# A fused attention and expert kernel: its program ordered by a model of the engines inside the kernel, and two blocks that take d_ff in halves

## The chip, the cores and the metric

The kernel runs on one core of a Trainium2 chip. The metric is device time in microseconds (us), the median of several runs. The engines named below: PE (TensorE, matrix products), DVE (VectorE), ACT (ScalarE), POOL (GpSimd), and SP, whose queue issues most of the transfers (DMAs).

## The reference

Attention in which keys and values are first averaged over groups of 8 positions, then an expert layer whose activation is a rational function:

```python
# attention: q, k, v are (8, 8, 576, 64): images, heads, positions, head size
k_p = k.reshape(B, H, Sp, 8, D).mean(axis=3)        # 72 pooled positions
v_p = v.reshape(B, H, Sp, 8, D).mean(axis=3)
scores = scale * np.matmul(q, k_p.transpose(0, 1, 3, 2))
scores = scores - np.max(scores, axis=-1, keepdims=True)
attn = np.exp(scores)
attn = attn / (np.sum(attn, axis=-1, keepdims=True) + 1e-09)
x = np.matmul(attn, v_p)       # laid out as 4608 tokens x 512
# expert: w_in 512 x 2048, w_out 2048 x 512 (both arrive as 8-byte floats)
h = x @ w_in
P = a[0] + a[1]*h + a[2]*h*h + a[3]*h*h*h
Q = 1.0 + np.abs(b[0])*np.abs(h) + np.abs(b[1])*h*h
out = (P / (Q + 1e-6)) @ w_out
```

## The kernel before

*Tiling.* The 4608 tokens are 18 blocks of 256, d_ff is 8 slices of 256. A unit (i, u) is block i with slice u, 144 in all. Products are made in three passes of a high and a low part (high x high, low weights x high, high weights x low), so `mm1` (L403) is 24 matmuls into one bank `ph`, and `mm2` (L448) 12 matmuls of 512 columns into the two banks `po` of the block's output, which gather over all 8 slices.

*Between them* `rational` (L414) computes the activation of a unit: three ACT reads (L421 to L423), a POOL product (L424), two DVE operations on `ph` (L425, L426), Ln and Exp on ACT into the bank `rp` (L432, L433), three DVE operations (L434, L436, L438), then the split into `gh` (ACT, L440) and `gl` (POOL, L441). mm2 of a unit stands LAG = 3 units behind its mm1.

*Weights.* `fetch` and `fetch_out` load 1 MB for each slice of w_in and w_out; `decode` (L160) turns 8-byte floats into a high and a low part with two ACT, two DVE (L168, L171) and one POOL operation per tensor (L166, L176, L177). A slice's two tensors are called a pair of weights below.

*Attention.* Per image, `prep_k` pools k (DVE, L233) and `prep_v` pools v (POOL, L199, L202; masks by ACT and DVE, L275 to L284). Per block, `attention` runs twice, on 128 tokens each: transposes of q (pq, L323), scores (ps, L338) with maximum and subtraction on DVE, exponential, sum and reciprocal, scaling (L352), the remainder `er` (L360, L361), transposes `pm` and `pr`; then `values` (L379) makes x in a high and a low part.

*Order.* The start, until block 0's x, is written out by hand in `tc.manual_schedule()` (L519 to L559). After that the units are emitted in the order of the list `order` (L564): blocks 0 and 1 together, block 1 two slices behind block 0, through all 8 slices, then block after block. Beside each unit a share of the next block's preparation and attention is emitted (`background`), and during block 0 the decoding of the slices ahead; a scheduler of the language then orders each engine's instructions when the program is built. At run time each engine takes its instructions in that order.

Of the kernel before, what the change touches and what calls it, by code (L numbers as in the profile page):

```python
# [13 lines left out]
AX = mybir.AxisListType  # L14


@with_exitstack
def tile_pooled_attention_then_rational_moe(
# [43 lines left out]
    ps_a = ctx.enter_context(tc.tile_pool(name="ps_a", bufs=2, space=PS))
# [16 lines left out]
    def make_masks():
# [15 lines left out]
        bands = tmp.tile([P, 4], F32, tag="tmp", name="bands")  # L95
# [20 lines left out]

    def make_scalars():
        for i in range(4):
            nc.gpsimd.tensor_scalar(out=abn[:, i:i + 1], in0=ab[:, i:i + 1],
                                    scalar1=-WS ** -i, scalar2=None, op0=ALU.mult)  # L120
        nc.scalar.activation(abn[:, 4:6], ab[:, 4:6], AF.Abs)

# [9 lines left out]


# [4 lines left out]
    def stage_tile(name, at=None):  # L138
        if at is None:
            return stage.tile([P, 1024], F32, tag="st", name=name)  # L140
        if at // 2 not in halves:
            halves[at // 2] = cpool.tile([P, 2, CW], F32, tag=spare[at // 2], name=name)
        return halves[at // 2][:, at % 2, :]

    w_in32, w_out32 = w_in.bitcast(I32), w_out.bitcast(I32)
    raw, win, wout = {}, {}, {}

    def fetch(u):
        w = raw[f"win{u}"] = cpool.tile([P, 2 * CW], F32, tag=f"win{u}", name=f"rwin{u}")
        nc.sync.dma_start(  # L150
            w.bitcast(I32).rearrange("p (k x) -> p k x", x=4 * P),
            w_in32[:, u * 4 * P:(u + 1) * 4 * P].rearrange("(k p) x -> p k x", p=P))

    def fetch_out(u):
        w = raw[f"wout{u}"] = cpool.tile([P, 2 * CW], F32, tag=f"wout{u}", name=f"rwout{u}")
        nc.sync.dma_start(
            w.bitcast(I32).rearrange("p (f x) -> p f x", f=2),
            w_out32[u * 2 * P:(u + 1) * 2 * P, :].rearrange("(f p) x -> p f x", p=P))

    def decode(kind, u):  # L160
        name = f"{kind}{u}"
        words = raw.pop(name).bitcast(I32).rearrange("p (n t) -> p n t", t=2)
        hw, lw = words[:, :, 1], words[:, :, 0]
        m = dec.tile([P, CW], F32, tag="m", name=f"m_{name}")
        mi = m.bitcast(I32)
        nc.scalar.activation(m, hw.bitcast(F32), AF.Prelu, scale=2.0 ** -111, alpha=-2.0 ** 32)  # L166
        yield
        nc.vector.tensor_scalar(out=mi, in0=mi, scalar1=3, scalar2=None,  # L168
                                op0=ALU.logical_shift_left)
        yield  # L170
        nc.vector.scalar_tensor_tensor(out=mi, in0=lw, scalar=29, in1=mi,  # L171
                                       op0=ALU.logical_shift_right, op1=ALU.bitwise_or)
        yield
        w = cpool.tile([P, 2, CW], F32R, tag=name, name=name)
        (win if kind == "win" else wout)[u] = w
        nc.scalar.copy(w[:, 0, :], m)  # L176
        nc.gpsimd.tensor_tensor(out=w[:, 1, :], in0=m, in1=w[:, 0, :].bitcast(F32),  # L177
                                op=ALU.subtract)
        yield

    def load_win(u):
        return decode("win", u)

    def load_wout(u):
        return decode("wout", u)


    kpT = [cpool.tile([P, NJ, 2 * SP], F32, tag=f"kpT{i}", name=f"kpT{i}") for i in range(2)]
    vm = [[cpool.tile([P, NJ, P], F32R, tag=f"vm{s}{i}", name=f"vm{s}{i}")
           for s in range(2)] for i in range(2)]  # L190
    vr = [cpool.tile([P, NJ, D], F32R, tag=f"vr{i}", name=f"vr{i}") for i in range(2)]
    for i in range(2):
        nc.gpsimd.memset(kpT[i], 0.0)

    def pool_rows(dst, st):

        w = st.shape[2] // 2
        while w > D:
            nc.gpsimd.tensor_tensor(  # L199
                out=st[:, :, 0:w], in0=st[:, :, 0:w], in1=st[:, :, w:2 * w], op=ALU.add)  # L200
            w //= 2
        nc.gpsimd.tensor_tensor(  # L202
            out=dst, in0=st[:, :, 0:w], in1=st[:, :, w:2 * w], op=ALU.add)

    def place(n, ks, j0, j1):

        pk = ps_a.tile([P, j1 - j0, SP], F32, tag="pa", name=f"pk{n}_{j0}")
        for j in range(j0, j1):
            nc.tensor.transpose(
                pk[:, j - j0, :], ks[:, 2 * j:2 * j + 2, :].rearrange("s h d -> s (h d)"),  # L210
                ident[:SP, :SP])
        for hh in range(2):
            rows = slice(hh * D, (hh + 1) * D)
            nc.scalar.activation(
                kpT[n % 2][rows, j0:j1, hh * SP:(hh + 1) * SP], pk[rows], AF.Copy,
                scale=1.0 / G)

    def prep_k(n):
        ks = tmp.tile([P, H * D], F32, tag="tmp", name=f"ks{n}")[:SP].rearrange("s (h d) -> s h d", h=H)

        def load(j):
            st = stage_tile(f"st_k{n}_{j}", j if n == 0 else None)
# [6 lines left out]
        if n == 0:  # L229
            yield  # L230
# [13 lines left out]
    def prep_v(n):  # L244
# [21 lines left out]
        if n == 0:  # L266
            yield
# [391 lines left out]
```

## Time and profile before

| | us |
|---|---|
| median of 3 runs (1034.76 to 1035.42) | 1034.84 |
| the profiled execution | 1034.07 |
| its span, first to last instruction | 1032.1 |

| engine | busy us | share of the span |
|---|---|---|
| PE | 970.7 | 94% |
| DVE | 796.0 | 77% |
| ACT | 703.6 | 68% |
| POOL | 537.7 | 52% |

Busy is the time in which an engine had an instruction in work; the ends of matmuls are modelled, so consecutive ones overlap a little. The granted clock is the share of PE's full clock that it was given: 0.964 on average. Transfers moved 48.24 MB in and 9.44 MB out. "Idle before" in a group is the time in which the engine stood before these instructions, with what released it.

### The profile page before, as it was taken

Reading aid. Unit: us, or ns where it says so; the run is one execution under the profiler, and the core shown is the slowest. Engines: PE = TensorE matmul, PEld = TensorE weight load, DVE = VectorE, ACT = ScalarE, POOL = GpSimd, SP = SyncE. Lnnn points to the kernel's source line nnn. Section 1 sums busy time; section 2 is a strip of 40 time slices with the busy share of each in tenths; the row PEclk is TensorE's granted clock in tenths of the full one; section 3 lists DMA queues with packets and bytes.
Section 4 is the critical chain, followed back from the end, with each engine's and each line's share of the span. In section 5 each row is a group of like instructions: output and inputs, shape, how many; then the busy total and the mean of one; then the engine's idle time right before and its main releaser. Section 6 shows DMA issues by size and latency. Waiting matters only on the chain.

```text
span 1032.1 us, 16779 instructions
## 1 busy us (share of the span) xinstructions
PE 970.7 (94%) x6324; PEld 880.5 (85%) x6324; DVE 796.0 (77%) x1232; ACT 703.6 (68%) x1218; POOL 537.7 (52%) x456
## 2 busy tenths in 40 slices
PE   5746599979999999999999999999999999999998
PEld 5635499969999999999999999999999989999997
DVE  6799966687779876878876978698869885867564
ACT  3664766657866876766776677677767776767664
POOL 5577945255535743535753465347534743444443
PEclk9677699989999999999999999999999999999999
DMA  8952100131002300002300230013002200000000
GB/s 237 414 192 64 44 21 2 42 105 44 22 21 68 82 21 22 22 21 65 85 21 22 64 85 22 21 65 85 21 22 64 63 21 21 22 1 21 1 22 21
DMA packets 61872, 58.75 MB, mean 57 GB/s; under 512 B 40288, under 2 KB 40288, under 8 KB 61792
## 3 DMA queue, kind: packets, MB, share of 16 engines
q1 hardware_dynamic: 61792, 57.69, 18.3%
q8 instruction: 50, 0.82, 0.3%
q14 instruction: 30, 0.25, 0.1%
HBM read 48.24 MB, written 9.44 MB: 56 GB/s over the span
## 4 chain that ended last, share of the span: by engine, by line
PE 87%; DVE 7%; DMA 2%; issue 2%; POOL 1%; ACT 1%; SPq 0%; POOLq 0%; ACTq 0%
PE po L457 38%; PE ph L409 38%; PE pv L394 4%; PE ps L338 4%; DVE ks L233 2%; PE pq L323 1%; DMA rwout<-in_moe_w_out_dram 1%; PE pm L366 1%; DVE m_wout L171 1%; DMA st_v<-in_v_dram 1%; DVE er L361 1%; DVE m_win L171 0%; POOL st_v L199 0%; DVE t L438 0%; DVE m_win L168 0%
## 5 line engine op out<-in xcount | busy, mean ns | idle before, releaser
L409 PE MATMUL ph<-x,win 128*128 128x256 f32 x3456 | 460.7, 287 | 9.3 <-POOL win L177 3.4
L409 PEld LDWEIGHTS ph<-x,win 128*128 128x128 f32 x3456 | 442.5, 191 | 23.4 <-issue 4.3
L457 PE MATMUL po<-wout,gh 128*128 128x512 f32 x1152 | 369.9, 404 | 20.0 <-ACT gh L440 20.0
L424 POOL TENSOR_TENSOR w<-w,r 128x512 f32<-128x512 f32 x144 | 194.3, 1349 | 329.9 <-ACT r L423 322.7
L457 PEld LDWEIGHTS po<-wout,gh 128*128 128x128 f32 x1152 | 210.3, 191 | 60.2 <-ACT gh L440 21.8
L441 POOL TENSOR_TENSOR gl<-t,gh 128x512 fp32r<-128x512 f32 x144 | 193.1, 1341 | 98.5 <-issue 59.0
L457 PE MATMUL po<-wout,gl 128*128 128x512 f32 x576 | 228.0, 401 | 3.7 <-POOL gl L441 3.6
L434 DVE SCALAR_TENSOR_TENSOR w<-w,rp 128x512 f32<-128x512 f32 x144 | 98.3, 682 | 117.2 <-ACT rp L433 115.7
L432 ACT ACTIVATE rp<-w,cbias 128x512 f32<-128x512 f32 x144 | 99.9, 694 | 87.7 <-POOL w L424 81.7
L421 ACT ACTIVATE w<-ph 128x512 f32<-128x512 f32 x144 | 86.3, 599 | 89.3 <-PE ph L409 88.3
L457 PEld LDWEIGHTS po<-wout,gl 128*128 128x128 f32 x576 | 109.6, 190 | 29.5 <-POOL gl L441 5.1
L425 DVE TENSOR_TENSOR t<-t,ph 128x512 f32<-128x512 f32 x144 | 98.0, 681 | 43.1 <-ACT t L422 41.6
L440 ACT CAST gh<-t 128x512 fp32r<-128x512 f32 x144 | 89.4, 621 | 53.9 <-DVE t L438 53.4
L423 ACT ACTIVATE r<-w,abn 128x512 f32<-128x512 f32 x144 | 118.6, 823 | 2.1 <-POOL gl L441 2.0
L422 ACT ACTIVATE t<-ph,abn 128x512 f32<-128x512 f32 x144 | 112.2, 779 | 1.6 <-POOL gl L441 1.6
L438 DVE SCALAR_TENSOR_TENSOR t<-w,t 128x512 f32<-128x512 f32 x144 | 110.5, 768 | 2.2
L426 DVE SCALAR_TENSOR_TENSOR t<-t,abn,ph 128x512 f32<-128x512 f32 x144 | 106.8, 742 | 2.3
L436 DVE SCALAR_TENSOR_TENSOR t<-t,abn,rp 128x512 f32<-128x512 f32 x144 | 106.5, 740 | 0.0
L433 ACT ACTIVATE rp<-rp 128x512 f32<-128x512 f32 x144 | 84.0, 584 | 3.2
L199 POOL TENSOR_TENSOR st_v<-st_v 128x512 f32<-128x512 f32 (+1 forms) x48 | 54.9, 1148 | 23.8 <-DMA st_v<-in_v_dram 22.9
L233 DVE TENSOR_REDUCE ks<-st_k 72x128 f32<-72x1024 f32 x32 | 62.4, 1974 | 1.6 <-DMA st_k<-in_k_dram 1.6
L338 PE MATMUL ps<-kpT,qT 128*128 128x144 f32 (+1 forms) x320 | 48.1, 294 | 4.6 <-DVE e L343 3.8
(70 smaller groups left out, 863.8 us busy)
## 6 DMA issues: line engine op xcount, KB each, us to landing
st_k<-in_k_dram SPq DMA_DIRECT2D x32, 288.0 KB
out_dram<-ob SPq DMA_DIRECT2D x36, 256.0 KB
qt<-in_q_dram SPq DMA_DIRECT2D x32, 256.0 KB
st_v<-in_v_dram SPq DMA_DIRECT2D x16, 512.0 KB
rwin<-in_moe_w_in_dram SPq DMA_DIRECT2D x8, 1024.0 KB
rwout<-in_moe_w_out_dram SPq DMA_DIRECT2D x8, 1024.0 KB
st_v<-in_v_dram SPq DMA_DIRECT2D x64, 64.0 KB
qt<-in_q_dram SPq DMA_DIRECT2D x8, 128.0 KB
```

Source lines behind the costliest of these rows:

```text
L409: nc.tensor.matmul(ph[:, f, :], lhsT=win[u][:, wi, (2 * c + f) * P:(2 * c + f + 1) * P], rhs=xs[xi][:, c, :], start=s == 0, stop=s == len( ...
L422: nc.scalar.activation(t, h, AF.Identity, bias=na2, scale=na3)
L423: nc.scalar.activation(r, w, AF.Identity, bias=b0, scale=b1)
L424: nc.gpsimd.tensor_tensor(out=w, in0=w, in1=r, op=ALU.mult)
L425: nc.vector.tensor_tensor(out=t, in0=t, in1=h, op=ALU.mult)
L426: nc.vector.scalar_tensor_tensor(out=t, in0=t, scalar=na1, in1=h, op0=ALU.add, op1=ALU.mult)
L432: nc.scalar.activation(r, w, AF.Ln, bias=cbias)
L434: nc.vector.scalar_tensor_tensor(out=w, in0=w, scalar=QC, in1=r, op0=ALU.add, op1=ALU.mult)
L436: nc.vector.scalar_tensor_tensor(out=t, in0=t, scalar=na0, in1=r, op0=ALU.add, op1=ALU.mult)
L438: nc.vector.scalar_tensor_tensor(out=t, in0=w, scalar=-2.0, in1=t, op0=ALU.add, op1=ALU.mult)
L441: nc.gpsimd.tensor_tensor(out=glf, in0=t, in1=ghf.bitcast(F32), op=ALU.subtract)
L457: nc.tensor.matmul(po, lhsT=g[:, f, ms], rhs=wout[u][:, wi, f * DM:(f + 1) * DM], start=(u == 0 and f == 0 and s == 0), stop=(u == NU - 1 ...
```

## The change

1. *Emission is split from order.* Every tile becomes a placeholder (`Lazy`, `Buf`) in a ring of buffers (`Ring`), and every operation an `Op` with an engine, a modelled cost, its dependencies and a due time. `Plan.solve` runs a list schedule over PE, DVE, ACT, POOL, SP and ACT's DMA issue: at each step the engine that can start first takes, among its operations that can start within 0.02 us of its earliest, the one due first. `Plan.issue` then emits the whole program in that order, all of it in `tc.manual_schedule()`. Costs: DVE 0.16 us + 1.04 ns per element, ACT 0.17 + 0.85, POOL 0.45 + 1.72, mm1 in six pieces of four matmuls of 119.5 ns, mm2 in six of two of 233 ns; a handoff between engines 0.07 us; DMA 360 bytes per ns in one line, plus 1.9 us. POOL's operations and DVE's marked `port` are held apart. An operation may start at most 24 us before it is due (DMAs 60, one kind 10).
2. *Blocks 0 and 1 take slices 0 to 3 first.* Their x is written to DRAM (`spill`), as are the partial sums of their output; blocks 2 and 3 follow, slices 0 to 3 of both and then 4 to 7 of both; then x comes back (`reload`), and blocks 0 and 1 take slices 4 to 7, with the partial sum added at the end.
3. *Due times*: unit number at is due at 30 + 8.6 us for each of the first 8 units, + 6.3 for each later one.
4. *Smaller changes.* `rp` lies with attention's banks for units of blocks 0 to 3 except the second half of 0 and 1; L434's result goes into `rp` in place and L436 goes ahead of it, so that L438's successor reads one operand from PSUM; mm2 runs over the two output banks innermost; `ks`, `vs`, `qT` have buffers of their own; the output of a block is one tile of 256 rows, with the decoder's buffers, and one DMA; the eight small loads of the first v go out on ACT's queue, and the remainder of v is loaded first; L352 is on POOL for every tile.

```diff
+    def add(self, eng, cost, calls, port=False, claims=(), bytes=0, early=24.0, after=()):
...
+    def solve(self):
+        for op in reversed(self.ops):
+            for d in op.deps:
+                d.users.append(op)
+                d.due = min(d.due, op.due - 1.6 * d.cost - 0.4)
+        for op in self.ops:
+            op.wait, op.ready = len(op.deps), max(0.0, op.due - op.early)
...
+                for op in cands:
+                    t = max(at[e], op.ready)
+                    if op.port:
+                        t = max(t, port)
...
+                t0 = min(t for t, _ in opts)
+                t, op = min(((t, op) for t, op in opts if t <= t0 + 0.02),
+                            key=lambda x: (x[1].due, x[1].seq))
+                if best is None or t < best[0]:
+                    best = t, op
...
+            op.start, op.end = t, t + op.cost
+            at[op.eng] = op.end
+            if op.port:
+                port = op.end
+            if op.bytes:
+                bus = max(bus, op.end) + op.bytes / 360e3
+                op.end = bus + 1.9
...
+    pool("dec", 2, loose=True)
+    pool("rat", 5)
+    pool("work3", 3)
+    pool("ps_o", 4, loose=True, space=PS)
+    pool("ps_h", 2, space=PS)
+    pool("ps_a", 2, loose=True, space=PS)
+    pool("hbm", 1, space=bass.MemoryType.DRAM)
...
+    dve = Engine(plan, "dve", 0.16, 1.04)
+    act = Engine(plan, "act", 0.17, 0.85)
+    gp = Engine(plan, "pool", 0.45, 1.72)
...
-        nc.vector.scalar_tensor_tensor(
-            out=w, in0=w, scalar=QC, in1=r, op0=ALU.add, op1=ALU.mult)
-        nc.vector.scalar_tensor_tensor(
-            out=t, in0=t, scalar=na0, in1=r, op0=ALU.add, op1=ALU.mult)
-        nc.vector.scalar_tensor_tensor(
-            out=t, in0=w, scalar=-2.0, in1=t, op0=ALU.add, op1=ALU.mult)
+        dve(W + 50).scalar_tensor_tensor(
+            out=t, in0=t, scalar=na0, in1=rp, op0=ALU.add, op1=ALU.mult)
+        dve(W).scalar_tensor_tensor(
+            out=rp, in0=w, scalar=QC, in1=rp, op0=ALU.add, op1=ALU.mult)
+        dve(W).scalar_tensor_tensor(
+            out=t, in0=rp, scalar=-2.0, in1=t, op0=ALU.add, op1=ALU.mult)
...
+    order = [(0, 0), (0, 1), (1, 0), (0, 2), (1, 1), (0, 3), (1, 2), (1, 3)]
+    order += [(i, u) for u0 in (0, NA) for i in (2, 3) for u in range(u0, u0 + NA)]
+    order += [(i, u) for i in range(2) for u in range(NA, NU)]
+    order += [(i, u) for i in range(4, NBLK) for u in range(NU)]
+    HEAD, PACE, SLOW, SLOWS = 30.0, 6.3, 8.6, 2 * NA
...
+    for at, (i, u) in enumerate(order):
+        again = i < 2 and u >= NA
+        plan.now = due(at)
+        if (i, again) not in xs:
+            xs[i, again] = reload(i, kept.pop(i)) if again else attend(i)
+            if i < 2 and not again:
+                kept[i] = spill(i, xs[i, again])
+        if ("win", u) not in weights:
+            load_weights("win", u)
+        ph = mm1(i, u, xs[i, again])
+        plan.now = due(at + LAG)
+        gh, gl = rational(i, u, ph)
+        if ("wout", u) not in weights:
+            load_weights("wout", u)
+        mm2(i, u, gh, gl)
+    plan.solve()
```

More of the change, by code (lines that the diff above doesn't have):

```diff
@@ new lines, in meet, with __init__, real @@
+def meet(a, b):
+    return all(x0 < y1 and y0 < x1 for (x0, x1), (y0, y1) in zip(a, b))
+class Buf:
+    def __init__(self, ring, shape, dtype, name):
+        self.ring, self.shape, self.dtype, self.name = ring, shape, dtype, name
+        self.writes, self.reads, self.left, self.held, self.it = [], [], 0, False, None
+    def real(self):
+        if self.it is None:
+            self.it = self.ring.pool.tile(self.shape, self.dtype, tag=self.ring.tag,
+                                          name=self.name)
+        return self.it
@@ new lines, in tile_pooled_attention_then_rational_moe, with new, bank @@
+    pool("stage", 2)
+    pool("work1", 1)
+    pool("work2", 2)
+    pool("dec", 2, loose=True)
[5 more added lines that the diff above has]
+    pool("hbm", 1, space=bass.MemoryType.DRAM)
+    def new(where, tag, shape, dtype, name):
+        return plan.tile(*pools[where], shape, dtype, tag, name)
+    def bank(where, name, shape):
+        return new(where, where, shape, F32, name)
@@ new lines, in tile_pooled_attention_then_rational_moe, with pe, mm, dma @@
+    dve = Engine(plan, "dve", 0.16, 1.04)
+    act = Engine(plan, "act", 0.17, 0.85)
+    gp = Engine(plan, "pool", 0.45, 1.72)
+    def pe(ns, calls, claims=(), after=()):
+        return plan.add("pe", ns / 1000, calls, claims=claims, after=after)
+    def mm(out, lhsT, rhs, start, stop):
+        return "matmul", (out,), dict(lhsT=lhsT, rhs=rhs, start=start, stop=stop)
+    def dma(kbytes, dst, src, eng="sp", issue=0.45, early=60.0):
+        plan.add(eng, issue, [("dma_start", (dst, src), {})], bytes=kbytes * 1024, early=early)
@@ L163, in decode @@
         hw, lw = words[:, :, 1], words[:, :, 0]
-        m = dec.tile([P, CW], F32, tag="m", name=f"m_{name}")
+        m = new("dec", "m", [P, CW], F32, f"m_{name}")
         mi = m.bitcast(I32)
[L166 to L203, printed above, removed]
@@ L205, in place @@
-    def place(n, ks, j0, j1):
[L207 to L211, printed above, removed]
+        act(CW).activation(m, hw.bitcast(F32), AF.Prelu, scale=2.0 ** -111, alpha=-2.0 ** 32)
+        dve(CW, port=True, rate=0.52).tensor_scalar(
+            out=mi, in0=mi, scalar1=3, scalar2=None, op0=ALU.logical_shift_left)
@@ new lines, in tile_pooled_attention_then_rational_moe @@
+    for n, at in ((8, 4.0), (14, 19.0)):
+        plan.now = at
+        pw = bank("ps_h", f"warm{n}", [P, P])
+        pe(220 * n, [mm(pw, ident, ident, True, True)] * n)
+    plan.now = 0.0
+    scalars()
+    xs, kept = {}, {}
+    for at, (i, u) in enumerate(order):
[13 more added lines that the diff above has]
+        mm2(i, u, gh, gl)
@@ L625, in tile_pooled_attention_then_rational_moe @@
-    while pend:
-        mm2(*pend.pop(0))
+        plan.issue()
 _INS = ["q", "k", "v", "moe_w_in", "moe_w_out", "moe_a", "moe_b"]
```

712 lines of the change are left out of this document (374 added, 338 removed).

## The prediction

> **What bounds the kernel now.** I read the span by slices first, then the busy time of each engine by stage, the chain, and the groups of VectorE's (DVE's) work early on.
>
> The page, with busy tenths in 40 slices of 25.8 us:
>
> ```profile
> span 1032.1 us, 16779 instructions
> PE   5746599979999999999999999999999999999998
> PEclk9677699989999999999999999999999999999999
> PE 87%; DVE 7%; DMA 2%; issue 2%; POOL 1%; ACT 1%; SPq 0%; POOLq 0%; ACTq 0%
> ```
>
> Busy time by stage (stage, length, then PE, weight load, DVE, ACT, POOL, clock, DMA share, GB/s):
>
> ```profile
> 0.00:32.00 32.00, 19.74 (x100) 16.72 (x100) 23.25 (x36) 12.72 (x26) 15.17 (x51) 0.90 0.86 271
> 32.00:60.00 28.00, 20.79 (x104) 18.49 (x104) 22.35 (x20) 19.20 (x26) 20.50 (x14) 0.75 1.04 396
> 60.00:140.00 80.00, 47.95 (x242) 41.12 (x243) 71.21 (x78) 49.18 (x75) 61.64 (x34) 0.72 0.20 60
> 140.00:250.00 110.00, 103.78 (x687) 94.02 (x686) 79.47 (x132) 70.86 (x128) 53.60 (x43) 0.95 0.18 50
> 250.00:1028.00 778.00, 778.00 (x5193) 710.18 (x5193) 599.47 (x970) 551.08 (x966) 386.83 (x316) 1.00 0.13 36
> ```
>
> From 250 us to the last matmul PE never idles, at clock 1.00. All there is to win lies before: from 60 to 140 us PE is busy 60% at clock 0.72 while DVE is busy 89%. To size it I price PE's whole work at full clock. The chain in order of time gives a unit (one block of 256 tokens times one 256-wide slice of d_ff):
>
> ```profile
> 1014.34 2.85 PE ph L409 x24
> 1017.18 11.25 PE po L457 x48
> ```
>
> mm1 is 2.85 us, mm2 11.25/4 = 2.81, a unit 5.66. PE's work after 250 us by tile, mm1 (ph), mm2 (po) and a transpose of attention (pm), counts in brackets:
>
> ```profile
> 250.00:1033.00 783.00, 376.65 (x2878) 1.00 0.13 37
> 250.00:1033.00 783.00, 371.43 (x1476) 1.00 0.13 37
> 250.00:1033.00 783.00, 16.78 (x112) 1.00 0.13 37
> ```
>
> 2878/24 = 120 mm1 and 1476/12 = 123 mm2 make 120 x 2.85 + 123 x 2.81 = 688 us; the other 90 of the 778 are attention of about 13.5 blocks (112/8 = 14 by pm, which runs early in a block, less a half), 6.7 each. The floor is 144 x 5.66 + 18 x 6.7 = 936 us. The last matmul ends at 1028.4 by these rows, so PE loses **92 us**, all in the first 250:
>
> ```profile
> 1028.03 0.40 PE L457 MATMUL po<-wout,gl 128*128 128x512 f32 x1
> 1028.25 1.16 SPq L470 DMA_DIRECT2D out_dram<-ob  x2
> ```
>
> The remaining 3.7 us to 1032.1 are the last drain and store.
>
> **Where the early loss comes from.** DVE's groups from 0 to 32 us, one image's pooling, block 0's attention and one decoded pair of weights:
>
> ```profile
> L233 DVE TENSOR_REDUCE ks<-st_k 72x128 f32<-72x1024 f32 x4 | 7.3, 1881 | 1.6 <-DMA st_k<-in_k_dram 1.6
> L352 DVE TENSOR_TENSOR e<-e,sm 128x576 f32<-128x576 f32 x1 | 1.6, 1600 | 0.0
> L276 DVE SCALAR_TENSOR_TENSOR vm<-vs,masks,vm 128x256 fp32r<-128x256 f32 x2 | 1.4, 740 | 0.9 <-ACT vm L275 0.9
> L171 DVE SCALAR_TENSOR_TENSOR m_win<-rwin,m_win 128x1024 int32<-128x1024 int32 x1 | 1.2, 1225 | 0.0
> L284 DVE SCALAR_TENSOR_TENSOR vr<-vs,masks,vr 128x128 fp32r<-128x128 f32 x2 | 0.6, 352 | 0.2 <-ACT vr L283 0.2
> L361 DVE TENSOR_TENSOR er<-e,er 128x64 fp32r<-128x64 f32 x4 | 1.0, 283 | 0.1
> L168 DVE TENSOR_SCALAR m_win<-m_win 128x1024 int32<-128x1024 int32 x1 | 0.7, 687 | 0.0
> ```
>
> And from 32 to 140 us:
>
> ```profile
> L171 DVE SCALAR_TENSOR_TENSOR m_wout<-rwout,m_wout 128x1024 int32<-128x1024 int32 x7 | 12.9, 1848 | 0.2
> L168 DVE TENSOR_SCALAR m_wout<-m_wout 128x1024 int32<-128x1024 int32 x7 | 10.1, 1438 | 1.5 <-ACT m_wout L166 1.5
> L438 DVE SCALAR_TENSOR_TENSOR t<-w,t 128x512 f32<-128x512 f32 x7 | 9.8, 1400 | 0.1
> L361 DVE TENSOR_TENSOR er<-e,er 128x64 fp32r<-128x64 f32 x4 | 4.9, 1234 | 0.0
> ```
>
> In those 108 us DVE finished 7 units (L438 x7) and decoded 7 pairs of weights, the last of which no unit needs before the end of this stage, and operations are stretched: 1438 ns for a shift of 687, 1234 for an er of 283. The whole-run groups of a unit, and the four ACT operations of a pair:
>
> ```profile
> L438 DVE SCALAR_TENSOR_TENSOR t<-w,t 128x512 f32<-128x512 f32 x144 | 110.5, 768 | 2.2
> L426 DVE SCALAR_TENSOR_TENSOR t<-t,abn,ph 128x512 f32<-128x512 f32 x144 | 106.8, 742 | 2.3
> L436 DVE SCALAR_TENSOR_TENSOR t<-t,abn,rp 128x512 f32<-128x512 f32 x144 | 106.5, 740 | 0.0
> L434 DVE SCALAR_TENSOR_TENSOR w<-w,rp 128x512 f32<-128x512 f32 x144 | 98.3, 682 | 117.2 <-ACT rp L433 115.7
> L425 DVE TENSOR_TENSOR t<-t,ph 128x512 f32<-128x512 f32 x144 | 98.0, 681 | 43.1 <-ACT t L422 41.6
> L166 ACT ACTIVATE m_win<-rwin 128x1024 f32<-128x1024 f32 x8 | 9.3, 1162 | 5.6 <-DMA rwin<-in_moe_w_in_dram 2.3 <-POOL wout L177 1.9 <-POOL win L177 1.4
> L176 ACT CAST win<-m_win 128x1024 fp32r<-128x1024 f32 x8 | 8.3, 1043 | 2.2 <-DVE m_win L171 2.2
> ```
>
> Quiet prices for DVE: image 7.3 + 1.4 + 0.6 = 9.3; pair 2 x (0.69 + 1.23) = 3.8; unit 3.61, or 3.5 with L438 at L434's price; a block's attention is the rest of the first stage, 23.3 - 1.6 (L352) - 9.3 - 3.8 = 8.6.
>
> **The change, part by part.** (a) *Head.* Block 0's chain from k to x is the same work. First matmul of mm1 in the timeline:
>
> ```profile
> 32.19 1.22 PE L409 MATMUL ph<-x,win 128*128 128x256 f32 x4 [1.62 <-ACT win L176]
> 9.33 6.44 SPq L261 DMA_DIRECT2D st_v<-in_v_dram  x8
> ```
>
> Eight v pieces leave SP's queue for ACT's, so the weights behind them on SP can be issued up to 6.4 us sooner; on ACT the first use is the transposed k, so I bound the effect by -6.4 and +6.4 and take -1: mm1 starts at 31. L352 for the second tile leaves DVE (1.6) and queues on POOL behind the first tile's and the pooling of v; what that delays lies within the +6.4. PE has then done one attention, so the head loses 31 - 6.7 = 24 us (18 to 30).
>
> (b) *Until unit 8*, the first of block 2. Only pairs 0 to 3 are needed, where (0, 7), the old order's 13th unit, needs the eighth pair. DVE must do: image 1, 9.3; attention of blocks 1 and 2, 17.2; three pairs, 11.4; five finished units, 17.5; the first two operations of three more, 4.3: 60 us. At the 89% of 60:140 that takes 67 us; fully busy 60. PE needs 8 x 2.85 + 5 x 2.81 + 2 x 6.7 = 50. Loss 17 (10 at best). ACT is next: the steady stage's 551.08 over 121 units is 4.6 us a unit with its share of attention, so 37 for eight; three pairs add 3 x 2 x (1.16 + 1.04) = 13, and one more block's attention at most DVE's 8.6: 59, under the 67. So ACT stays hidden, with little room.
>
> (c) *Units 8 to 31*, until block 4. DVE: 24 x 3.5 + 17.2 + 9.3 + 4 pairs 15.2 = 126, at 89% 141 us; PE needs 24 x 5.66 + 13.4 = 149. PE is the bound again; pairs and image 2 come in lumps, so 3 us lost (0 to 15).
>
> (d) *Steady stage.* Same matmuls; mm2 alternates its two banks and mm1 is issued as six pieces that other work can go between. The trace has no row for alternation; with no PE idle in 778 us the nearest price is 0. A new fixed order can make PE stand as it once did when DVE pooled image 2's k ahead of block 3's er:
>
> ```profile
> 217.04 0.34 PE L374 MATMUL pr<-identr,er 128*128 128x128 f32 x1 [5.92 <-DVE er L361]
> ```
>
> Six images (2 to 7) are pooled beside the units from 24 on in the new order; a hole of 5.92 at half of them is 18 us, the high end; -5 is the low one, if the 6.7 of attention holds hidden waits. I take 2, near the 778 us without any.
>
> (e) *Extra transfers.* x of blocks 0 and 1 goes out and back (8 x 512 KB), partial sums out and back (4 x 512 KB): 6.3 MB, 16 us at the 396 GB/s of 32:60, in stages where DMA is 0.18 to 0.20 busy: hidden. On SP's queue each store waits for its producer, with loads behind it; they have up to 60 us of lead in the plan, and if that cover goes, block 0's second half waits for one reload, 1 MB, about 3 us at that rate and its latency. Four drains and the adds, about 5 us of DVE and ACT, lie in the saturated stage with DVE at 77%.
>
> (f) *PSUM.* L434 now writes in place and L438 reads one operand there: 0 to 0.09 us less per unit on DVE, in (b) already. rp stays one operation longer; its bank is shared with attention until block 3. Nothing by itself.
>
> (g) *Tail.* One 512 KB store after both halves instead of two of 256 KB: between 0 and +1.5, +0.7 taken: 4.4.
>
> Sum: 936 + 24 + 17 + 3 + 2 + 4.4 = 986.4 of span; outside its span the profiled execution spent 1034.07 - 1032.1 = 2.0, and it stands 0.8 under the median of the runs, 1034.84: 986.4 + 2.0 + 0.8 = **989 us**.
>
> **Rivals.** *The clock stays low.* PE's 50 us of (b) at the 0.72 of 60:140 take 70, about DVE's 67; if it lasts to unit 16, another 8 x 5.66 x (1/0.72 - 1) = 18: 989 + 3 + 18 = 1010. For it: 0.72 through a stage of 60% busy PE. Against: there the holes are long,
>
> ```profile
> 73.19 2.08 PE L457 MATMUL po<-wout,gh 128*128 128x512 f32 x4 [9.31 <-ACT gh L440]
> ```
>
> here 17 us over 8 units are 2 us each. The Trainium skill, "TensorE: Matmul & The Clock Gate", section "HAM oscillation — how this bites in real kernels", says to leave no PE gap above about 3.4 us, and Part 1 that PE falls to half rate after such a window. The 9.31 us hole beside 0.72 agrees; by that rule 2 us gaps would keep the clock whole and the sum at 989. Gaps gathered into lumps would by the same page give half rate: an estimate of 100 us for those 50, and 989 + 33 = 1022.
>
> *The stretching stays.* With the prices of 32:140 (pair about 5.6, L438 1.40, er 1.23 against 0.28), (b) costs DVE 60 + 3 x 1.8 + 5 x 0.7 + 8 x 0.95 = 77, at 89% 87: 20 more, and some 5 in (c): 1014. Against: the plan lets an operation it marks as sharing a port begin only when POOL is free.
>
> *DVE full.* (b) at 60, head at 28, nothing lost in (c) and (d): 989 - 7 - 3 - 5 = 974.
>
> *Slower.* All queues now run a fixed order built on modelled costs, 0.07 us per handoff. If PE's next instruction were late by a little in every unit, there is no other work it can take. It decides from 46/128 = 0.36 us per unit behind unit 16 on; at 0.5 the time is 989 + 64 = 1053. For it: a unit passes ACT, POOL and DVE several times each, and PE takes its instructions strictly in the planned order. Against: the old order is just as fixed when it runs, and PE had no idle in 778 us, with ACT at 71% and DVE at 77%, so a late unit can catch up.
>
> *No shift*: the plan may leave DVE's early order as crowded as it is, so no gain: 1030 to 1037.
>
> **Chances.** Forecast (980 to 1000 for itself) 0.52, since its two large terms come from rows of the same work; DVE full 0.16; clock low 0.10; stretched 0.10; slower 0.08; no shift 0.04. The range 968 to 1016 takes in the first four but for their outer ends, and leaves out the last two. A run here tells about 0.2%, 2 us, from no change. Faster: the first four and a quarter of the last, 0.89; within 0.2%: half of the last, 0.02; slower 0.09.
>
> **What would show it.** Right: mm1 of block 2 begins near 98 us (before, only 7 units were through DVE at 140); L168 near 0.7 us throughout; PE full from about 110 us, clock 1.00; L438's successor near 0.69; the steady stage without PE idle. Wrong: gaps in PE behind 250 us, a clock under 0.8 past 100 us, a first mm1 later than 36 us, or ACT rather than DVE ending the early waits.

## The result, and the profile after

The changed kernel takes **1011.4 us** (median of 4 runs, 1011.06 to 1011.94) where the kernel before took 1034.8 beside it (1034.68 to 1035.42): ratio 0.9773, interval 0.9756 to 0.979. The profiled execution took 1011.59, its span 1009.6. Faster, as forecast, and inside the range, but half of the gain foreseen: 23 us of 46.

The page of the changed kernel: its span, PE's tenths and granted clock in 40 slices of 25.2 us, the engines' shares of the chain that ended last, and one group of instructions (every planned instruction carries line L236, where the plan is issued):

```profile
span 1009.6 us, 16759 instructions
PE   5569899999999999999999999999999999999997
PEclk7679899999999999999999999999999999999999
PE 83%; DVE 7%; ACT 3%; DMA 2%; issue 2%; POOL 2%; POOLq 0%; ACTq 0%; SPq 0%
L236 DVE SCALAR_TENSOR_TENSOR t<-rp,t 128x512 f32<-128x512 f32 x144 | 99.2, 689 | 4.1
```

PE's row reaches its nines two slices sooner than before. But its first three slices stand at 5, 5, 6 under a clock of 7, 6, 7; before, the clock began with 9. The last line is L438's successor, 689 ns instead of 768. Busy time by stage, same columns as before:

```profile
0.00:32.00 32.00, 15.59 (x76) 13.51 (x76) 17.06 (x23) 8.08 (x18) 16.66 (x56) 0.69 0.96 279
32.00:60.00 28.00, 16.61 (x101) 14.40 (x101) 25.71 (x40) 19.88 (x31) 12.41 (x8) 0.74 0.70 216
60.00:140.00 80.00, 71.81 (x455) 62.29 (x456) 68.58 (x109) 56.79 (x98) 50.85 (x37) 0.91 0.43 152
140.00:250.00 110.00, 108.05 (x695) 96.59 (x695) 90.10 (x124) 89.37 (x140) 70.84 (x53) 1.00 0.28 78
250.00:1006.00 756.00, 750.95 (x5002) 679.49 (x5000) 571.17 (x942) 536.59 (x935) 367.05 (x306) 1.00 0.13 38
```

From 60 to 140 us PE is busy 71.81 us at clock 0.91, where it was busy 47.95 at 0.72: that is the gain. The first two stages give some of it back: 15.59 and 16.61 busy against 19.74 and 20.79.

To compare with the forecast's sum, this table puts the losses of PE in its terms: the start of a unit's first mm1 matmul in the timeline, less PE's work done by then at the forecast's prices (2.85, 2.81, 6.7 us), the work counted by matmuls (by 126.66 us, the start of unit 8 in the changed kernel: 8 mm1, 86 of mm2's matmuls, 24 transposes pm). Blocks of attention behind the head are the mean of two counts, 8 pm to a block and 21.3 pv (384 in all over 18 blocks). Good to some 2 to 4 us, as the before column's -3.6 shows.

| term, us | before | forecast | after |
|---|---|---|---|
| (a) head: first mm1 at | 32.2 | 31 | 42.6 |
| loss in the head | 25.5 | 24 | 35.9 |
| (b) further, until unit 8 | 59.6 | 17 | 27.7 |
| (c) until unit 32 | 10.9 | 3 | 0.4 |
| (d) until the last matmul | -3.6 | 2 | 5.4 |
| (g) tail | 3.7 | 4.4 | 4.2 |
| span with the floor of 936 | 1032.1 | 986.4 | 1009.6 |

The 23.2 us between forecast and result are (a) +11.9, (b) +10.7, (d) +3.4, (c) -2.6 and (g) -0.2. What the change gained is (b) and (c), 42 us against before; the head took 10 of it back, (d) by this count 9, of which the trace shows 5.05 us as idle time of PE behind 250 us.

**The head in the timeline.** Start and length in us, queue issues as SPq and ACTq, idle time and releaser in brackets:

```profile
0.81 9.34 ACTq L236 DMA_DIRECT2D st_v<-in_v_dram  x8
2.06 0.40 SPq L236 DMA_DIRECT2D st_k<-in_k_dram  x1
5.14 0.36 SPq L236 DMA_DIRECT2D ab<-in_moe_b_dram  x1
7.59 0.30 SPq L236 DMA_DIRECT2D st_k<-in_k_dram  x1
7.97 2.60 SPq L236 DMA_DIRECT2D qt<-in_q_dram  x2
13.97 1.11 PE L236 MATMUL pq<-identr,qt 128*128 128x128 f32 x4 [4.13 <-DMA qt<-in_q_dram]
14.50 1.26 POOL L236 TENSOR_TENSOR st_v<-st_v 128x512 f32<-128x512 f32 x1 [6.30 <-DMA st_v<-in_v_dram]
17.69 0.40 ACT L236 ACTIVATE vr<-vs,masks 128x128 fp32r<-128x128 f32 x1 [6.43 <-POOL vs L236]
18.11 0.58 ACT L236 COPY qT<-pq 128x512 f32<-128x512 f32 x1
18.84 1.30 PE L236 MATMUL ps<-kpT,qT 128*128 128x144 f32 x4 [3.76 <-ACT qT L236]
42.57 0.63 PE L236 MATMUL ph<-x,win 128*128 128x256 f32 x2
```

The eight small loads of v keep ACT's queue for 9.34 us; the plan costs them at 0.1 each. Most of that is waiting. Single issues (count, then ns min/median/max, first and last start in us), and the longest of SP's waits up to 16 us (us in total, times, longest):

```profile
L236 ACTq DMA_DIRECT2D st_v<-in_v_dram x8: 317/354/447, 0.8 to 9.8; - x8
SPq L236 <- DMA st_k<-in_k_dram: 6.8, 4, 2.7
```

In the records of the trace each of the program's 200 transfers carries one of eight semaphores (25 each), on whichever queue it goes out, and an issue whose semaphore is still in use waits until that transfer has landed. The first eight issues are out by 2.62 us, four of them v's. ACT's next goes out at 4.60, when its first load has landed (4.58). SP's issues stand still twice (2.46 to 5.14, 5.50 to 7.59), each time until a piece of k has landed (5.12, 7.57). So q goes out at 7.97 and is on PE at 13.97. The plan's model has no such limit.

The copy qT has to wait further, until 18.11: ahead of it on ACT stands vr, which waits for pooled v, the last piece of which left at 10.15. The plan had put vr there because by its costs v would be pooled just before q's transposes. Before, the first pq was at 8.93 and the first ps at 11.78.

Behind the first ps PE waits 4.57 us for the scaling e, now two in a row on POOL (3.64 us from 29.22 on), and 3.90 for a pair of er that take 2.46 us (from 35.77 on) beside POOL's win; with v on SP, below, such a pair takes 0.35.

### The profile page after: what moved, and what is told of

It reads as the page before. It is cut to its first block, busy times and chain, and to the rows that moved or that the text cites. A ratio compares the mean times of both kernels' runs of the same rounds, so it can differ in the third digit from the quotient of the medians.

```text
span 1009.6 us, 16759 instructions
## 1 busy us (share of the span) xinstructions
PE 963.0 (95%) x6324; PEld 866.3 (86%) x6324; DVE 772.6 (77%) x1235; ACT 710.7 (70%) x1218; POOL 517.8 (51%) x457
## 4 chain that ended last, share of the span: by engine, by line
PE 83%; DVE 7%; ACT 3%; DMA 2%; issue 2%; POOL 2%; POOLq 0%; ACTq 0%; SPq 0%
PE ph L236 37%; PE po L236 36%; PE pv L236 4%; PE ps L236 3%; DVE t L236 2%; DMA st_v<-in_v_dram 2%; DVE sm L236 1%; PE pm L236 1%; PE pq L236 1%; DVE m_wout L236 1%; ACT rp L236 1%; POOL w L236 1%; DVE e L236 1%; DVE mx L236 0%; PE pr L236 0%
## 5 line engine op out<-in xcount | busy, mean ns | idle before, releaser
L236 PEld LDWEIGHTS ph<-x,win 128*128 128x128 f32 x3264 | 465.0, 188 | 57.2 <-issue 5.5
L236 PE MATMUL ph<-x,win 128*128 128x256 f32 x3264 | 489.6, 283 | 3.2 <-DVE t L236 1.4
L236 PE MATMUL po<-wout,gh 128*128 128x512 f32 x1152 | 354.5, 401 | 3.9 <-ACT gh L236 2.4
L236 POOL TENSOR_TENSOR w<-w,r 128x512 f32<-128x512 f32 x144 | 187.6, 1303 | 267.7 <-ACT r L236 256.1
L236 POOL TENSOR_TENSOR gl<-t,gh 128x512 fp32r<-128x512 f32 x144 | 187.5, 1302 | 139.9 <-ACT gh L236 116.9
L236 PEld LDWEIGHTS po<-wout,gh 128*128 128x128 f32 x1152 | 189.5, 191 | 20.1 <-ACT gh L236 3.9
L236 PE MATMUL po<-wout,gl 128*128 128x512 f32 x576 | 183.9, 400 | 0.3 <-POOL gl L236 0.2
L236 DVE TENSOR_TENSOR t<-t,ph 128x512 f32<-128x512 f32 x144 | 98.2, 682 | 83.1 <-ACT t L236 79.9
L236 DVE SCALAR_TENSOR_TENSOR t<-t,abn,rp 128x512 f32<-128x512 f32 x144 | 106.9, 743 | 59.4 <-ACT rp L236 57.3
L236 ACT ACTIVATE w<-ph 128x512 f32<-128x512 f32 x144 | 85.8, 596 | 93.1 <-PE ph L236 88.7
L236 ACT ACTIVATE t<-ph,abn 128x512 f32<-128x512 f32 x144 | 109.4, 768 | 25.7 <-PE ph L236 25.7
L236 ACT ACTIVATE r<-w,abn 128x512 f32<-128x512 f32 x144 | 117.4, 816 | 10.4 <-DVE rp L236 3.3
L236 ACT ACTIVATE rp<-w,cbias 128x512 f32<-128x512 f32 x144 | 99.4, 690 | 30.9 <-POOL w L236 22.6
L236 ACT CAST gh<-t 128x512 fp32r<-128x512 f32 x144 | 88.4, 614 | 34.5 <-DVE t L236 33.6
L236 DVE SCALAR_TENSOR_TENSOR t<-t,abn,ph 128x512 f32<-128x512 f32 x144 | 107.2, 744 | 6.3 <-ACT w L236 2.5
L236 DVE SCALAR_TENSOR_TENSOR t<-rp,t 128x512 f32<-128x512 f32 x144 | 99.2, 689 | 4.1
L236 PEld LDWEIGHTS po<-wout,gl 128*128 128x128 f32 x576 | 93.8, 190 | 8.1 <-POOL gl L236 1.6
L236 DVE SCALAR_TENSOR_TENSOR rp<-w,rp 128x512 f32<-128x512 f32 x144 | 99.1, 688 | 0.0
L236 ACT ACTIVATE rp<-rp 128x512 f32<-128x512 f32 x144 | 84.0, 584 | 3.2
L236 DVE TENSOR_REDUCE ks<-st_k 72x128 f32<-72x1024 f32 x32 | 63.8, 1997 | 4.9 <-DMA st_k<-in_k_dram 4.8
L236 POOL TENSOR_TENSOR e<-e,sm 128x576 f32<-128x576 f32 x36 | 42.5, 1190 | 31.8 <-DVE sm L236 27.5
L236 POOL TENSOR_TENSOR st_v<-st_v 128x512 f32<-128x512 f32 (+1 forms) x48 | 50.0, 1046 | 17.0 <-DMA st_v<-in_v_dram 16.3
```

The source lines that it names most:

```text
L236: getattr(engines[op.eng], name)(*map(value, args), **{k: value(v) for k, v in kw.items()})
```

## The experiments

All times are medians against the kernel before on the same chip (1034.5 to 1034.7 us in each set); differences between two versions are of medians. Unit starts are from the timelines. Wherever the program is planned anew, its whole order changes with the one thing edited: a single difference of a few us may be the order's.

**Where v is issued (planned anew each time).** First, 1.17 us for an issue, the mean of the 9.34 us on ACT's queue (a price for issue and wait together):

```diff
-                            **(dict(eng="act", issue=0.1) if n == 0 else {}))
+                            **(dict(eng="act", issue=1.17) if n == 0 else {}))
```

> One number of the planner changes: the eight loads of the first v on ACT's queue are given the 1.17 us each that the changed kernel's trace shows (9.34 us for eight) instead of 0.1; they stay on that queue, and the whole order is planned anew. Theory A (the head is late because ACT's instructions were ordered for loads that cost nothing: two vr copies stand ahead of qT and wait for the pooled v): the first mm1 starts at 35 to 38 us instead of 42.6, qT no longer waits for vr, and the time falls by 4 to 8 us, to 1003 to 1007. Rival B (the head is late by the slow PE clock, the masks on POOL and the late q, none of which this touches): first mm1 at 41 or later, time 1008 to 1015.

Measured 1016.02 us (1015.58 to 1016.45), ratio 0.9819 (0.9803 to 0.9836): outside both. qT came at 14.73 instead of 18.11 and the first mm1 3 us sooner (39.5), yet the time rose by 4.6: unit 8 was 3.5 us sooner, but units 8 to the end lost 11 us against 6. A new cost makes a new order everywhere, and the plan made with this one ends later by its own count as well (1003 us against 996), so this run doesn't price the issue. Second, v on SP's queue:

```diff
-                            **(dict(eng="act", issue=0.1) if n == 0 else {}))
+                            **{})
```

> The same eight loads go out on SP's queue at the planner's usual 0.45 us each, as the kernel before had them on SP; planned anew. Theory A: ACT is free from about 2 us, kpT is copied near 8 us instead of 10.3, first mm1 at 34 to 38 us, time 1000 to 1006. Rival B: first mm1 at 40 or later, time 1008 to 1015. If SP's queue, which now has eight more loads ahead of the weights, is the limit instead, the decoding of the first weights ends later than x and mm1 waits for a weight, not for x.

Measured **1001.41 us** (1000.33 to 1002.02), ratio 0.9678 (0.9664 to 0.9693): 10.0 us less, a time in the first theory's range, with a first mm1 (38.23) just outside it. Its head in the timeline:

```profile
2.50 0.38 SPq L236 DMA_DIRECT2D ab<-in_moe_b_dram  x1
2.92 0.39 SPq L236 DMA_DIRECT2D st_k<-in_k_dram  x1
3.35 1.02 SPq L236 DMA_DIRECT2D qt<-in_q_dram  x2
4.59 11.12 SPq L236 DMA_DIRECT2D st_v<-in_v_dram  x10
11.91 0.59 ACT L236 COPY qT<-pq 128x512 f32<-128x512 f32 x1 [1.82 <-PE pq L236]
38.23 1.27 PE L236 MATMUL ph<-x,win 128*128 128x256 f32 x8
```

q is now among the first eight transfers and goes out 4.6 us sooner (of the 11.12 us behind it, one issue alone took 5.02), qT is 6.2 us sooner, mm1 4.3. By unit 8 the loss was 5.8 us less (57.8 against 63.6 in all), at the last matmul 11.1 less. So some 6 of the 10 us arise before unit 8, the rest later, in an order that is also a new one.

**The halves of d_ff.** Blocks 0 and 1 take all eight slices at once, block 1 two slices behind, as before; no spill, reload or partial sums, and rp lies with attention's banks for blocks 0 and 1 alone; once on the changed kernel, once with v on SP:

```diff
-    NA = NU // 2
+    NA = NU
-    order = [(0, 0), (0, 1), (1, 0), (0, 2), (1, 1), (0, 3), (1, 2), (1, 3)]
-    order += [(i, u) for u0 in (0, NA) for i in (2, 3) for u in range(u0, u0 + NA)]
-    order += [(i, u) for i in range(2) for u in range(NA, NU)]
-    order += [(i, u) for i in range(4, NBLK) for u in range(NU)]
+    order = []
+    for s in range(NU + 2):
+        if s < NU:
+            order.append((0, s))
+        if s >= 2:
+            order.append((1, s - 2))
+    order += [(i, u) for i in range(2, NBLK) for u in range(NU)]
```

> The planner alone: blocks 0 and 1 take all eight slices as before the change, block 1 two slices behind block 0, then block after block; nothing is spilled or reloaded, and rp of blocks 2 and 3 lies in the output's banks. Theory C (postponing four pairs of weights saves DVE 4 x 3.8 us ahead of unit 8 and little else): 1015 to 1022, so most of the 23 us gained come from the planned order. Rival D (the halves carry the gain, the planner only makes them possible): 1028 to 1036.

> The planner without the halves (as in e3_no_halves) and with the first v's small loads on SP's queue (as in e2_v_on_sp), to weigh the halves where the head no longer disturbs the planned order. Theory C (the halves save little): 1004 to 1010 against e2's 1001.4, so 3 to 9 us. Rival D (the halves carry the gain once the plan holds): 1016 or more.

Measured 1015.93 us (1015.22 to 1020.12; ratio 0.9828, 0.9808 to 0.9849) and 1006.48 (1004.33 to 1006.99; 0.9723, 0.971 to 0.9736): the halves are worth 4.5 and 5.1 us. Without them unit 8 began sooner (108.7 us against 126.7, and 95.1 against 119.0 with v on SP), since it needs no attention of block 2, but the pairs for slices 4 to 7 then press: the loss grew from 60.1 at unit 8 to 71.5 at unit 12, from 46.5 to 56.6 on the other base. So of the 23 us the new order of units carries about 5. The rest is the plan together with the smaller changes, which no run takes apart.

**Holding POOL and DVE apart.** The planner's rule for operations marked as sharing a port is taken out, on both bases:

```diff
-                    if op.port:
-                        t = max(t, port)
```

> The planner no longer holds POOL's operations and DVE's marked ones apart; its order packs them closer, and its own plan ends 14.5 us sooner (981 us instead of 996). Theory E (the stretched operations are a lock that a plan has to respect): DVE's shift and er are stretched again, above 1.0 us and above 0.5 us in the first 140 us, and the time is 1008 to 1020, no gain. Rival F (holding them apart costs more than the lock itself, since DVE and POOL stand idle for each other): 995 to 1004.

> No holding apart of POOL and DVE's marked operations (as in e4_no_port), with the loads on SP's queue. In e2_v_on_sp the stretched operations are nearly gone (er 0.23 us, shifts 0.69 and 0.96 between 32 and 140 us); in e4_no_port they are back (second decode operation 2.26 us). Theory E: stretched again, no gain over e2: 1000 to 1010, although its own plan ends 12 us sooner than e2's. Rival F: 986 to 995.

Measured 1014.02 us (1012.29 to 1014.36; ratio 0.9798, 0.9783 to 0.9813) and 1010.97 (1010.29 to 1011.57; 0.9771, 0.9757 to 0.9784): 2.6 and 9.6 us slower than their bases, the first hardly more than the 2 us that runs tell apart. DVE is busy longer from 32 to 140 us, 97.6 us for 94.3 and 97.1 for 90.0. Its groups from 32 to 140 us without the rule, v on SP:

```profile
L234 DVE TENSOR_TENSOR er<-e,er 128x64 fp32r<-128x64 f32 x12 | 8.8, 773 | 0.1
L234 DVE SCALAR_TENSOR_TENSOR m_wout<-rwout,m_wout 128x1024 int32<-128x1024 int32 x4 | 6.1, 1530 | 0.0
L234 DVE TENSOR_SCALAR m_wout<-m_wout 128x1024 int32<-128x1024 int32 x4 | 4.6, 1162 | 0.0
```

With the rule, first that base, then the changed kernel itself:

```profile
L236 DVE TENSOR_TENSOR er<-e,er 128x64 fp32r<-128x64 f32 x14 | 2.7, 228 | 1.4 <-ACT er L236 1.4
L236 DVE SCALAR_TENSOR_TENSOR m_wout<-rwout,m_wout 128x1024 int32<-128x1024 int32 x4 | 4.9, 1218 | 0.0
L236 DVE TENSOR_SCALAR m_wout<-m_wout 128x1024 int32<-128x1024 int32 x4 | 3.8, 955 | 0.0
```

```profile
L236 DVE TENSOR_TENSOR er<-e,er 128x64 fp32r<-128x64 f32 x14 | 7.6, 580 | 0.4 <-ACT er L236 0.4
L236 DVE TENSOR_SCALAR sm<-sm 128x8 f32<-128x8 f32 x6 | 3.9, 657 | 0.2
```

With the rule most of the stretching is gone on this base (er 228 ns; 283 in the quiet stage before), not all: the shift of m_wout takes 955, where 687 is its quiet price. In the changed kernel er still takes 580 (383 without the rule on that base); that its run lags its plan by more, and so puts instructions beside each other that the plan held apart, fits this but wasn't tried alone. The 128x8 operation on sm isn't marked as sharing at all.

**Due times.** With v on SP, the first 8 units due sooner and closer:

```diff
-    HEAD, PACE, SLOW, SLOWS = 30.0, 6.3, 8.6, 2 * NA
+    HEAD, PACE, SLOW, SLOWS = 18.0, 6.3, 7.0, 2 * NA
```

> As e2_v_on_sp, with the due times 18 + 7.0 us per early unit instead of 30 + 8.6. Its own plan ends at 990 us instead of 995 and has unit 8 begin at 106 instead of 111. Theory G (with the loads on SP the chip follows the plan, within 4 us at its end): 995 to 998. Rival H (plan and chip agreed in e2 by chance, the chip has its own floor in the early stage): 1000 to 1004.

Measured **999.98 us** (999.11 to 1002.28), ratio 0.9668 (0.9655 to 0.9681): the fastest of all, but its runs overlap those of its base. Unit 8 began 2.6 us sooner, the last matmul 0.3. And, with v on SP, block 2's attention alone due 20 us sooner:

```diff
         if (i, again) not in xs:
+            plan.now = due(at) - (20 if i == 2 else 0)
             xs[i, again] = reload(i, kept.pop(i)) if again else attend(i)
+            plan.now = due(at)
```

> As e2_v_on_sp, with block 2's pooling and attention due 20 us sooner, nothing else changed. It asks whether the 25 us lost between units 0 and 8 come from placing block 2's x behind all eight early units. Theory I (DVE and POOL are full in this stage, so what is pulled forward delays the first units by as much): unit 8 some 7 us sooner, unit 4 later, end 1001 to 1007 (the plan itself ends 5 us later). Rival J (the stage is lost by order, not by work): 992 to 997.

Measured 1008.63 us (1008.02 to 1011.32), ratio 0.9753 (0.974 to 0.9767): 7.2 slower. Unit 8 began 8.4 us sooner (110.6), and the loss at that point was 53.6 instead of 57.8; at unit 16 it was still 4 us less (52.9 against 56.9), at unit 24 (215.0 us) 61.2 against 56.9. All that was won, and 4 us more, came back between units 16 and 24. So unit 8's start is not by itself what the order has to win.

**The changed kernel's order kept, single things moved.** Here nothing is planned anew. First, qT of tile 0 ahead of the vr on ACT:

```diff
     plan.solve()
+    order = plan.order
+    vr = next(op for op in order if op.eng == "act" and any(b.name == "vr0" for b in op.bufs))
+    qT = next(op for op in order if op.eng == "act" and any(b.name == "qT0" for b in op.bufs))
+    order.remove(vr)
+    order.insert(order.index(qT) + 1, vr)
```

> The changed kernel with the same planned order but for one move: on ACT's queue the copy qT of tile 0 goes ahead of the vr it stood behind (17.69 us, waiting for POOL's pooled v). pq ends at 15.1, qT started at 18.11. Theory M (that order on ACT sets the head): qT at about 15.1, first mm1 at 39 to 40 us, time 1007 to 1009. Theory N (the next late arrival takes its place: pooled v, er, or the work of DVE and POOL before unit 8 that a sooner start does not shorten): first mm1 over 41 us or no gain in time, 1010 to 1013.

Measured 1009.15 us (1007.59 to 1009.75), ratio 0.9752 (0.9739 to 0.9765). The first mm1 was 1.4 us sooner (41.2), unit 8 and the last matmul 2.5; it lies between the two theories, and 2.3 us less of time are little more than runs tell apart. The head gained less than the 3 us of the move, since pq came 0.6 later in that run and PE then stood 1.38 us for kpT. Second, that move, and the eight loads issued by SP behind the first two of q:

```diff
+    loads = [op for op in order if op.eng == "act" and op.calls[0][0] == "dma_start"]
+    q1 = next(op for op in order if op.eng == "sp" and any(b.name == "qt1" for b in op.bufs))
...
+        op.eng = "sp"
...
```

POOL's first sum over these loads, which reads them, moves behind them too.

> As the run before (qT ahead of vr on ACT), and also the eight small loads of v are issued by SP behind the first two loads of q instead of by ACT; all else in the changed kernel's planned order, so nothing is planned anew. The version planned anew with v on SP had qT at 11.91, first mm1 at 38.2 and 1001.4 us. Theory M (issue and order in the head carry that version's gain): qT at 12 to 13.5, first mm1 at 36 to 39, time 1002 to 1007. Theory O (most of that gain came from the rest of the new order, or is taken back in the stage that DVE fills): first mm1 sooner but time 1008 to 1012.

Measured 1010.25 us (1008.48 to 1011.5), ratio 0.9764 (0.9751 to 0.9777). The time is within 1.2 us of the changed kernel's, in the second theory's range, though that too had expected a sooner mm1. SP issued as in the version planned anew (q at 3.35), but mm1 stayed at 42.4. Its ACT and PE rows:

```profile
13.84 0.59 ACT L236 COPY qT<-pq 128x512 f32<-128x512 f32 x1 [3.48 <-PE pq L236]
19.70 0.40 ACT L236 ACTIVATE vr<-vs,masks 128x128 fp32r<-128x128 f32 x1 [5.27 <-POOL vs L236]
20.00 0.57 ACT L236 ACTIVATE kpT<-pk 64x144 f32<-64x144 f32 x2
20.62 1.33 PE L236 MATMUL ps<-kpT,qT 128*128 128x144 f32 x4 [4.52 <-ACT kpT L236]
```

qT is 4.3 us sooner, but the same vr, now later because v goes out behind q, stands on ACT for 5.27 us with kpT behind it, and PE waits 4.52 for that. So it is not the issue alone: the order on ACT has to know when v comes. The version planned anew had qT at 11.91, this kpT at 13.53, and vr after 25 us.

Last, the clock of the head: in every stretch from 8 us to the first mm1 that the plan leaves PE idle, warm-up matmuls fill it (they write a bank that nobody reads), with v on SP and the sooner due times, and on the changed kernel:

```diff
...
         for op in self.order:
+            if op.eng == "pe":
+                fill = fill and op is not self.first
+                if fill and at > 8.0:
+                    for _ in range(int((op.start - at) / 0.109)):
+                        self.nc.tensor.matmul(self.warm.ap(), lhsT=self.ident, rhs=self.ident,
+                                              start=True, stop=True)
+                at = op.end
```

> Base: the version with v on SP's queue and due times 18 + 7.0 per unit (999.98 us); same plan and same order, but in every stretch ahead of block 0's first mm1 in which the plan leaves PE idle, warm-up matmuls of 128 columns are put on PE to fill it (0.109 us each), as the kernel before had 28 of them at 17.47 us. In the base the granted clock is 0.50 from 16 to 36 us, where the kernel before had 1.00 until 24. Theory J (the head is long because the changed kernel does all its warming up in the first 9 us and the clock then falls): clock near 1.00 through 36 us; PE's 16 us of transposes, scores and values between 12 and 38 us take about half, of which 3 to 5 us lie on the path: first mm1 at 33 to 35 us (base 37.7), time 994 to 998. Theory K (the head is set by transfers, POOL and DVE; PE's half clock lies in waits): first mm1 at 37 or later, time 999 to 1003, more if the inserted matmuls stand in the way of ready ones.

> The changed kernel, same plan and order, with the same filling of PE's planned idle time ahead of block 0's first mm1. There the granted clock is 0.55 from 12 to 16 us and 0.50 from 16 to 40. Its first mm1 is at 42.6 us. J: clock near 1.00, first mm1 at 38 to 40, time 1006 to 1010. K: 42 or later, time 1010 to 1014.

Measured 1013.0 us (1012.51 to 1013.11; ratio 0.9791, 0.9777 to 0.9804) and 1021.6 (1018.67 to 1022.18; 0.9869, 0.9856 to 0.9883): 13.0 and 10.2 us slower than their bases, outside the ranges of both theories (the second had allowed the first run more if fillers stood in the way of ready work). The clock did stay at 1.00 from 8 to 44 us in the first. But the plan's idle time is not the chip's. PE in the base, then with the filling:

```profile
12.07 0.73 PE L236 MATMUL ps<-kpT,qT 128*128 128x144 f32 x4 [1.07 <-ACT kpT L236]
12.63 0.29 PE L236 MATMUL pk<-identr,ks 72*128 72x72 f32 x2
13.59 1.33 PE L236 MATMUL ps<-kpT,qT 128*128 128x144 f32 x4 [0.67 <-ACT kpT L236]
```

```profile
12.16 0.73 PE L244 MATMUL ps<-kpT,qT 128*128 128x144 f32 x4 [1.07 <-ACT kpT L244]
12.72 5.30 PE L240 MATMUL warm<-identr 128*128 128x128 f32 x46
17.86 0.29 PE L244 MATMUL pk<-identr,ks 72*128 72x72 f32 x2
```

pk, ready at once in the base, stands behind 46 fillers. What the half clock costs the head by itself thus stays open; it wasn't tried with fewer. The two runs do measure something else: the head became 11.6 and 9.9 us longer, and the last matmul came 12.9 and 9.8 us later.

| same order, us | first mm1 | unit 8 | last matmul |
|---|---|---|---|
| changed kernel | 42.6 | 126.7 | 1005.4 |
| qT ahead of vr | 41.2 | 124.1 | 1002.9 |
| both moved | 42.4 | 126.9 | 1005.4 |
| filled | 52.5 | 136.7 | 1015.1 |

Under a fixed order a delay of 10 us in the head comes out at the end about one for one; of the small moves, 1.4 us sooner gave 2.5, and 0.2 gave nothing.

## Why the prediction was right, and where its terms were wrong

*The mechanism* was right in part. The early stage had been bound by DVE, and more than half of its loss went (59.6 to 27.7). But of the two reasons in (b), fewer pairs and DVE at its quiet prices, the first carries only about 5 us. The version without halves and with v on SP shows the second: from 32 to 140 us DVE was busy 93.5 us, as before the change (93.6), and decoded the same seven pairs, but finished 12 units instead of 7. Two of its rows there, for 1400 and 1438 ns before:

```profile
L236 DVE SCALAR_TENSOR_TENSOR t<-rp,t 128x512 f32<-128x512 f32 x12 | 8.3, 690 | 0.3
L236 DVE TENSOR_SCALAR m_wout<-m_wout 128x1024 int32<-128x1024 int32 x7 | 4.8, 687 | 0.0
```

The forecast had put the quiet prices into its sum and argued for them only against a rival, by the plan's rule. Most of the gain goes with them; what share the rule, the order and L438's operand in PSUM have in that is open. (c), (g), (e) and (f) came out as put: 0.4 and 4.2 us lost, no wait for spilled x, L438's successor at 689 ns as forecast. With (a) and (b) both over by more than 10 us, it is the width of the range, 48 us, that takes the result in, 4.6 us from its end.

*Step (a) failed*, by 11.9 us. It took the eight loads on ACT for between -6.4 and +6.4 us, and bounded a delay by SP's old 6.44 us. They kept ACT's queue for 9.34 us, 3.0 of them issues and the rest waits for one of the eight semaphores; and as they held four of the first eight, SP's loads of q waited too (out at 7.97, before at 2.51). And, what the forecast didn't ask, a plan that knows neither this limit nor the wait puts a waiting vr ahead of qT. That "block 0's chain is the same work" was true of its work, not of its order. Its sign to watch for, a first mm1 later than 36 us, was there. How the 11.9 splits isn't settled. Against the kernel before, 7.1 of 10.4 us are there at the first ps (18.84 for 11.78); behind it lie the waits for e and er, which the moves of single things left as they were (4.57 and 3.91). Planning anew with v on SP gave back 4.3 us of head, moving qT alone 1.4; part may lie in the clock.

*Step (b) was mis-sized*, 27.7 us for 17. From the first mm1 to unit 8 the trace has

```profile
42.57:126.66 84.09, 69.48 (x432) 59.39 (x432) 72.87 (x115) 60.82 (x103) 52.35 (x37) 0.90 0.51 174
```

DVE was busy 87% of it, close to the 89% assumed; but with 72.87 us of work, not 60. Its groups in that stretch show what was left out: all 8 units finished, not 5 and part of 3 (8 x 3.5 = 28 against 21.8), five tiles of attention and the start of a sixth instead of four (26.4 against 17.2 by its eight groups, er at 473 ns and sm at 566 among them; rows of consecutive instructions overlap, so such sums come out high, 78.9 over all groups for 72.87), four m_wout decoded where three pairs were counted (14.0 against 11.4). The forecast assumed that at unit 8 the finishing would lag; in the plan's order block 2's x comes last of all, behind the units. The clock was 0.90, not 1.00, a part of the same loss.

*Step (d)*: PE idle 5.05 us of the 756 behind 250 us, where 2 were taken and 18 bounded it; PE's longest sums of waits from 140 to 1006 us (us in total, times, longest):

```profile
PE po L236 <- ACT gh L236: 2.0, 3, 1.0
PE ph L236 <- DVE t L236: 1.6, 3, 1.1
```

No hole of the feared 5.92 us, and no wait for a reload of x.

*The rivals.* The slower case, a little late in every unit, fell: from unit 32 on 5.4 us are lost in 112 units, 0.05 each against the 0.36 from which it decides. The stretching stayed in part: if the plan does nothing against it, the port experiments say 2.6 to 9.6 us more, new orders included. The clock: from 60 to 140 us it was 0.91, so not the rival as worked out, but in 0 to 60 us it was 0.69 to 0.74, and nothing in the forecast's head allowed for that. The kernel before had 28 warm-up matmuls at 17.47 us; the new plan lets all 44 go in the first 9 us, since their due time of 19 us less the 24 that an operation may start early is below zero. The forecast's head has no term for this.

On the clock the forecast cited the Trainium skill, "TensorE: Matmul & The Clock Gate", section "HAM oscillation — how this bites in real kernels", for gaps above about 3.4 us. The rows of the filling experiment's base speak against using that as the only limit, though they don't show what the clock counts as idle (pq and pk between them are transposes): four ps matmuls of one shape go from 0.73 to 1.33 us between 12.07 and 13.59, with no idle time of PE over 1.07 us since the warm-up ended at 9.14. PE was busy 1.14, 0.78 and 1.26 us of the three 2 us stretches from 8 on:

```profile
8.00:10.00 2.00, 1.14 (x11) 0.94 (x9) 2.00 (x3) 0.00 (x0) 0.21 (x1) 1.00 1.07 178
10.00:12.00 2.00, 0.78 (x6) 0.64 (x6) 1.71 (x1) 1.05 (x3) 0.59 (x4) 1.00 0.88 236
12.00:14.00 2.00, 1.26 (x8) 1.15 (x9) 0.92 (x2) 0.57 (x2) 0.54 (x2) 0.83 1.02 250
14.00:16.00 2.00, 1.77 (x8) 1.36 (x7) 0.92 (x2) 0.00 (x0) 1.71 (x3) 0.50 0.43 68
```

## What to carry to other kernels

A program ordered on a model is as good as the model's cheapest wrong entry in the part where one chain decides: compare the plan's cost of each kind of instruction with the trace's, take a long issue apart into work and wait before giving it a price, ask which limits the model lacks (here the transfers in flight), then look for the instruction that waits ahead of one that is ready. A sooner milestone (unit 8 here) is no gain while the engine behind it is full; count that engine's whole work up to there, the finishing included. And after any edit of a planner's input the whole order is new: a single effect is measured by moving things in the order that stands.

## What the runs showed of the hardware that was not expected

A queue that looks busy may be waiting. The eight loads of 64 KB that kept ACT's queue for 9.34 us took 0.32 to 0.45 us each to issue; the first, out at 0.81, had landed at 4.58, and only then could the fifth go. With the same loads on SP behind q, otherwise in almost the same order, q's issue was at 3.35 instead of 7.97. The Trainium skill, "DMA: Bandwidth & Descriptors", section "Issuing engines are not separate DMA queues", says that issuing from several engines only saves the issue time on the sequencer, usually small beside the transfer. The trace agrees: 0.39 us of issue against 3.77 us until that load had landed.

A DVE operation on 128x8 that takes 0.17 us alone took 2.01 us beside POOL's 2.37 us one, and both ended at 41.9 us (the version with the sooner due times):

```profile
39.89 2.01 DVE L236 TENSOR_SCALAR sm<-sm 128x8 f32<-128x8 f32 x1
39.49 2.37 POOL L236 TENSOR_TENSOR win<-m_win,win 128x1024 fp32r<-128x1024 f32 x1 [6.55 <-ACT win L236]
```
